# One store per output tile, a held-back score stretch and a last tile in three pieces

## The chip, the core and the metric

The kernel runs on one core of one Trainium2 chip. The core has TensorE (PE in the profile, with its weight loads as PEld), VectorE (DVE), ScalarE (ACT), GpSimd (POOL) and SyncE (SP), and 16 DMA engines. The metric is the device time of one execution in microseconds (us), lower is better. Before the change it is 586.98 us, the median of three runs (586.29 to 587.70).

## What is computed

Attention over 8 batches, 12 heads, 448 tokens and a head width of 64, with queries and keys divided by their root mean square and scaled by gains; then a mixer of rank 32 along the tokens; then a feed-forward layer along the 768 channels. All inputs and the output are 32-bit.

```
q_n, k_n = rmsnorm(q, g_q), rmsnorm(k, g_k)
attn = softmax(q_n @ k_n.T / 8)
x = (attn @ v) with the heads side by side        # 8 x 448 x 768
u = x + (x.T @ U @ V).T                            # U: 448 x 32, V: 32 x 448
out = u + relu(u @ w_ch1) @ w_ch2                  # 768 -> 3072 -> 768
```

## The kernel before, in words

**The work.** Matrix products take 16-bit operands. Twenty-four groups of four heads (`gi`, three to a batch) are loaded, normalised and turned so that the head width lies on the partitions. The last eighteen groups are turned by DMA transposes (`turn_dma`, L376), whose queries GpSimd then multiplies by the gains (`take_dma`, L383). A pair of heads (`pr`, six to a batch) has its scores and exponentials made by `Spair` (L422), in seven 128-key blocks: two blocks and one more each take a buffer of the PSUM pool `ps` (four buffers), two double blocks take the pool `ps_sc`. `V` (L448) multiplies by the values.

**The feed-forward part.** For each batch: `mix_t`, `mix_tr` and `mix_rows` (L479, L489, L525) make `u`, four DMA transposes (L548) bring it to `uT`, 24 `up` steps (L550) make `hT`, and `down` (L579) makes the output. A tile of output has 128 rows: two runs of 64 tokens, each at a stride of seven tokens in DRAM. It is made in two halves of 384 channels, each of 24 matmuls in four parts of six, and VectorE adds `u` to each half. A tile is stored by two DMAs of 64 rows each, half tile by half tile in the first batch and as whole rows of 768 after it. The last tile of the last batch is one of these: two halves, then two stores.

**The order.** It is laid down by a loop at the end of the kernel that merges two lists, the attention (`att`) and the feed-forward part (`mlp`), each entry with a cost. It keeps an estimate of the time at which each engine will be done (`at`, moved on by `runs`), and issues the next attention entry when its due time has come and `ready` (from L845) agrees. Engines take their instructions in this order. All loads of the attention, all stores and all DMA transposes go through SP's one DMA queue. A mixer step that would come directly behind a score stretch is moved behind a `down` part (`after_pair`).

**Single things that the steps below use.** `load_u` (L299) and the load of V (L304), whose DRAM side is V read four times over, for four groups of 32 partitions:

```
nc.sync.dma_start(Vf, moe_V.rearrange("(m r) s -> m r s", m=1).to_broadcast([NQ, rank, S]))   # NQ = 4
```

`sums` (L161) are two reductions on VectorE that the attention list puts into its queue once per group.

Of the kernel before, what the change touches and what calls it, by code (L numbers as in the profile page):

```python
# [9 lines left out]
FP32 = mybir.dt.float32  # L10
# [3 lines left out]
ALU = AluOpType  # L14
# [12 lines left out]
def kernel(  # L27
# [13 lines left out]
    nc = tc.nc  # L41
    B, H, S, D = q.shape
    dm = H * D
# [3 lines left out]
    P = 128  # L47
    NT = S // 64
    NJ = S // P
    SM = NJ * P  # L50
    R = S - SM
# [6 lines left out]
    KH = dh // P  # L58
    NPAIR = H // 2
    HALF = dm // 2  # L60
# [9 lines left out]
    outp = ctx.enter_context(tc.tile_pool(name="outp", bufs=3))  # L70
    ps_sc = ctx.enter_context(tc.tile_pool(name="ps_sc", bufs=2, space=bass.MemoryType.PSUM))
    ps = ctx.enter_context(tc.tile_pool(name="ps", bufs=4, space=bass.MemoryType.PSUM))
# [3 lines left out]
    for b in range(B):  # L76
        h = 0
# [194 lines left out]
    w2b = consts.tile([P, KH, dm], BF16)  # L272
    hT = consts.tile([P, KH, 512], BF16)
# [21 lines left out]
    Uf = first[:, 2, :2 * (NJ + 2) * rank].bitcast(FP32).rearrange("p (j r) -> p j r", r=rank)  # L295
    nc.gpsimd.memset(Uf[:, NJ:, :], 0.0)
    Urows = moe_U.rearrange("(p j) r -> p j r", j=NT)

    def load_u():  # L299
        for i in range(2):  # L300
            nc.sync.dma_start(Uf[i * R:(i + 1) * R, :NJ, :], Urows[:, i * NJ:(i + 1) * NJ, :])
        nc.sync.dma_start(Uf[R:P, NJ, :], Urows[:, 2 * NJ, :])
        nc.sync.dma_start(Uf[0:R, NJ + 1, :], Urows[:, 2 * NJ, :])
        nc.sync.dma_start(Vf, moe_V.rearrange("(m r) s -> m r s", m=1).to_broadcast([NQ, rank, S]))  # L304
# [32 lines left out]
    at = {"pe": 0.0, "act": 0.0, "dve": 0.0}  # L337
    exp_done = {}

    def runs(eng, us):  # L340
        at[eng] = us + (at["pe"] if eng == "pe" else max(at["pe"], at[eng]))

    qk, es, xs = {}, {}, {}
# [136 lines left out]
    def mix_t(b):  # L480

        pt = ps.tile([P, KD, rank], FP32, name="pu", tag="ps")
        for dt in range(KD):
            for j in range(NW):
                nc.tensor.matmul(pt[:, dt, :], xs[b][:, j, dt * P:(dt + 1) * P], Ub[:, j if j < NJ else NJ + b % 2, :],  # L485
                                 start=(j == 0), stop=(j == NW - 1))
        nc.vector.tensor_copy(tb_bufs[b % 2][:, :KD * rank], pt.rearrange("p k r -> p (k r)"))

    def mix_tr(b):  # L489
        pt = ps.tile([P, 2, P], BF16, name="pw", tag="ps")  # L490
        for i in range(2):
            nc.tensor.transpose(pt[:, i, :], tb_bufs[b % 2][:, i * P:(i + 1) * P], ident)
        tTs[b] = headp.tile([P, 2, P], BF16, name="tT", tag="tT")
        nc.vector.tensor_copy(tTs[b], pt)

    def mix_t0(lo, hi, scalar=False):

        pt = ps.tile([P, 512], FP32, name="pu0", tag="ps")
        for j in range(NW):
            nc.tensor.matmul(pt[:, :hi - lo], Uz[:, j, :], xs[0][:, j, lo:hi], start=(j == 0), stop=(j == NW - 1))  # L500
        if scalar:
            nc.scalar.copy(tz[:, lo:hi], pt[:, :hi - lo])
        else:
            nc.vector.tensor_copy(tz[:, lo:hi], pt[:, :hi - lo])
# [17 lines left out]
    def urows(b, col, half):  # L522
        h = slice(half * HALF, (half + 1) * HALF)
        return u_rest[:, h] if col == SM else xs[b][:, (col - (0 if b % 2 else R)) // P, h]
# [51 lines left out]

    down_ps, down_sb = {}, {}

    def down(b, col, half, part, nparts):  # L579
        key = (b, col, half)  # L580
        if part == 0:
            down_ps[key] = ps.tile([P, HALF], FP32, name="po", tag="ps")
        po = down_ps[key]
        n = KH // nparts
        for ht in range(part * n, (part + 1) * n):
            nc.tensor.matmul(po, hT[:, ht, col:col + P], w2b[:, ht, half * HALF:(half + 1) * HALF],  # L586
                             start=(ht == 0), stop=(ht == KH - 1))
        runs("pe", 0.98)
        if part < nparts - 1:
            return  # L590
        runs("dve", 0.55)
        h = slice(half * HALF, (half + 1) * HALF)
        if half == 0 or b == 0:
            down_sb[(b, col)] = outp.tile([P, dm], FP32, name="ob", tag="ob")
        ob = down_sb[(b, col)]
        nc.vector.tensor_tensor(ob[:, h], po, urows(b, col, half), ALU.add)  # L596
        if half == 1 or b == 0:
            h = h if b == 0 else slice(0, dm)

            def rows(b, j):  # L600
                return out[b].rearrange("(p j) d -> j p d", j=NT)[j]
            for i in range(2):
                o = rows(b, i * NJ + col // P) if col != SM else rows(b - i, 2 * NJ)
                nc.sync.dma_start(o[:, h], ob[i * R:(i + 1) * R, h])


    pairs = [(b, pr) for b in range(B) for pr in range(NPAIR)]
# [144 lines left out]
    mlp = []  # L752
    for b in range(B):
        for ht in range(KH):
            mlp.append((0.38, up_part, (b, ht, 4, KD), b) if b == 0 and ht < 2 else (1.14, up, (b, ht), b))
            if b < ROWS_FROM and ht % 2 == 0 and ht < 4 * NW:
                mlp.append((0.17, mix_rows, (b, ht // 4, ht // 2 % 2), b))
        cols = (64, 192, 320) if b % 2 == 0 else (384, 0, 128, 256)
        n = len(cols) * 8
        nb = b + 1  # L760
        pre = {}
        if ROWS_FROM <= nb < B:
            pre[n - PRE[nb > 1]] = [(0.77, mix_t, (nb,), nb)]
            pre[n - PRE[nb > 1] + 1] = [(0.11, mix_tr, (nb,), nb)]
            for piece in range(2 * NW):
                pre.setdefault(n - PRE[nb > 1] + 2 + (piece if nb > 1 else piece // 2), []).append(
                    (0.17, mix_rows, (nb, *divmod(piece, 2)), nb))
        tiles = [(col, half) for col in cols for half in range(2)]
        if b == 0:
            tiles.sort(key=lambda t: t[1])  # L770
        for c, (col, half) in enumerate(tiles):
            for part in range(4):
                mlp.extend(pre.get(c * 4 + part, []))
                mlp.append((0.98, down, (b, col, half, part, 4), b))

    a_, b_ = PARTS
    squares_part(0, *a_)
# [31 lines left out]
    sums(2, 0)  # L809
    stage_tiles(3)  # L810
    load_u()
    load_v(2)
    load_qk(3, 0)
# [28 lines left out]
    def mixes(f):  # L842
        return f in (mix_t, mix_tr, mix_rows)

    def ready(f, a):  # L845
        if f is Spair:
            return im == 0 or not mixes(mlp[im - 1][1])
        if ca >= a_one:
            return True
        if f is V:  # L850
            return exp_done[a[:2]] <= at["pe"] + 0.1
        return f is not Srows or at["act"] <= at["pe"] + 0.6

    later, turning, after_pair = [], False, False
    while ia < len(att) or im < len(mlp):
# [4 lines left out]
        if ia == a_from and im == 0:  # L860
            at.update(pe=0.0, act=0.0, dve=0.0)
        may_mlp = im < len(mlp) and ia >= done_at[mlp[im][3]]
        take_att = ia < len(att) and (not may_mlp or ca <= due(cm) and ready(*att[ia][1:]))
        if take_att:
            c, f, a = att[ia]
            if f is load:
                later.append((f, a))
            else:
                f(*a)
            after_pair = f is Spair or after_pair and f is not V  # L870
            if ia >= a_from:
                ca += c
            ia += 1
            if f is scale_all and a[0] < DMA_FROM:
                weights(2)
            if f is T and a == (DMA_FROM - 1, 1):
                nc.vector.memset(kp[:, 2 * NJ:], 0.0)
        else:
            if after_pair and mixes(mlp[im][1]):
                nb, n, moved = mlp[im][3], im, []  # L880
                while mixes(mlp[n][1]) and mlp[n][3] == nb:
                    e = next(i for i in range(n, len(mlp)) if mlp[i][1] is down)
                    moved += [mlp[e], *mlp[n:e]]
                    n = e + 1
                mlp[im:n] = moved
            after_pair = False
            c, f, a, _ = mlp[im]
            f(*a)
            turning = f is mix_t and a[0] > 0 or turning and a != (a[0], NW - 1, 1)
            cm += c  # L890
            im += 1
# [30 lines left out]
```

## Time and profile before

| what | value |
|---|---|
| median of three runs | 586.98 us (586.29 to 587.70) |
| the profiled execution's own time | 586.64 us |
| its span, first to last instruction | 584.8 us |
| PE busy | 572.2 us, 98% of the span |
| ACT, POOL, DVE busy | 307.9, 210.3, 196.8 us |
| moved by DMA | 68.21 MB, mean 117 GB/s |
| granted TensorE clock | 0.999 |

The page of the profile gives busy times, the span in 40 slices and the chain of work that ended last. The lists of waits say which engine stood idle and what ended it. The timeline shows instructions in order of time: start, length, engine, line, operation and how many were merged. The answer by windows gives for any stretch the busy time of each engine and, last, the mean busy share of the 16 DMA engines and the GB/s that they moved.

### The profile page before, as it was taken

Reading aid. Unit: us, or ns where it says so; the run is one execution under the profiler, and the core shown is the slowest. Engines: PE = TensorE matmul, PEld = TensorE weight load, DVE = VectorE, ACT = ScalarE, POOL = GpSimd, SP = SyncE. Lnnn points to the kernel's source line nnn. Section 1 sums busy time; section 2 is a strip of 40 time slices with the busy share of each in tenths; the row PEclk is TensorE's granted clock in tenths of the full one; section 3 lists DMA queues with packets and bytes.
Section 4 is the critical chain, followed back from the end, with each engine's and each line's share of the span. In section 5 each row is a group of like instructions: output and inputs, shape, how many; then the busy total and the mean of one; then the engine's idle time right before and its main releaser. Section 6 shows DMA issues by size and latency. Waiting matters only on the chain.

```text
span 584.8 us, 11725 instructions
## 1 busy us (share of the span) xinstructions
PE 572.2 (98%) x4826; PEld 338.2 (58%) x4826; DVE 196.8 (34%) x458; ACT 307.9 (53%) x510; POOL 210.3 (36%) x310
## 2 busy tenths in 40 slices
PE   8899999999999999999999999999999999999996
PEld 7555556555665555655556555665556655655563
DVE  6676656212352232521235231442034310410011
ACT  7866661677445776277653578457753344014200
POOL 5995684265314515334523433441531000000000
PEclk9999999999999999999999999999999999999999
DMA  8899999683546642585246735375204210420022
GB/s 229 170 241 241 244 233 231 119 220 52 133 78 167 153 106 35 139 212 130 36 122 109 180 104 123 66 172 149 35 25 92 48 28 1 68 61 1 1 54 55
DMA packets 104509, 68.21 MB, mean 117 GB/s; under 512 B 66568, under 2 KB 101256, under 8 KB 104456
## 3 DMA queue, kind: packets, MB, share of 16 engines
q1 hardware_dynamic: 95044, 58.03, 42.6%
q0 software_dynamic: 9408, 9.44, 9.6%
q8 instruction: 38, 0.62, 0.4%
q14 instruction: 15, 0.12, 0.1%
q10 hardware_dynamic: 4, 0.00, 0.0%
HBM read 52.20 MB, written 11.01 MB: 108 GB/s over the span
## 4 chain that ended last, share of the span: by engine, by line
PE 91%; DMA 3%; DVE 2%; POOL 1%; ACT 1%; issue 1%; SPq 1%; POOLq 0%; ACTq 0%
PE ph L554 36%; PE po L586 36%; PE pv L466 6%; PE sc L436 2%; PE sl L427 2%; PE sl L438 2%; PE pv L462 2%; PE pm L537 2%; DMA qf<-in_q_dram 1%; PE sc L415 1%; ACT E L416 1%; DMA vf<-in_v_dram 1%; DVE ssq L162 1%; DMA qT<-qn 1%; PE pu L485 1%
## 5 line engine op out<-in xcount | busy, mean ns | idle before, releaser
L586 PE MATMUL po<-w2b,hT 128*128 128x384 bf16 x1344 | 237.4, 326 | 0.0
L554 PE MATMUL ph<-uT,w1b 128*128 128x448 bf16 x1140 | 228.7, 352 | 0.0
L586 PEld LDWEIGHTS <-hT 128*128 128x128 bf16 x1344 | 126.8, 98 | 75.5 <-issue 0.6
L554 PEld LDWEIGHTS <-w1b 128*128 128x128 bf16 x1140 | 108.3, 98 | 93.8 <-issue 0.7
L561 ACT ACTIVATE hT<-ph 128x448 bf16<-128x448 f32 x184 | 98.0, 550 | 120.2 <-PE ph L554 118.9
L429 ACT ACTIVATE E<-sl,gg 128x448 bf16<-128x448 f32 x72 | 41.5, 629 | 75.9 <-PE sl L427 75.9
L386 POOL TENSOR_SCALAR qT<-qT,gg 128x448 bf16<-128x448 bf16 x36 | 50.5, 1402 | 81.6 <-DMA qT<-qn 65.2
L193 POOL TENSOR_TENSOR qn<-qf,rs 128x384 bf16<-128x384 f32 x36 | 29.9, 829 | 132.4 <-ACT rs L170 127.5
L469 DVE RECIPROCAL r<-pv 128x4 f32<-128x4 f32 x96 | 17.4, 182 | 167.8 <-PE pv L466 167.6
L441 ACT ACTIVATE E<-sc,gg 128x896 bf16<-128x896 f32 x72 | 69.0, 1022 | 0.0
L596 DVE TENSOR_TENSOR ob<-po,x 128x384 f32<-128x384 f32 x48 | 26.7, 557 | 103.8 <-PE po L586 103.4
L466 PE MATMUL pv<-va,E 128*128 128x65 bf16 x1152 | 57.1, 194 | 0.0
L466 PEld LDWEIGHTS <-E 128*128 128x128 bf16 x1152 | 50.5, 98 | 6.3
L162 DVE TENSOR_REDUCE ssq<-sq 128x14 f32<-128x896 f32 x45 | 46.8, 1078 | 2.4 <-ACT sq L140 2.3
L462 PE MATMUL pv<-vl,E 128*128 128x130 bf16 x192 | 42.2, 220 | 0.3 <-ACT E L416 0.2
L470 DVE TENSOR_TENSOR x<-pv,r 128x256 bf16<-128x256 f32 x96 | 40.7, 424 | 3.3
L416 ACT ACTIVATE E<-sc,gg 128x896 bf16<-128x896 f32 (+1 forms) x42 | 37.5, 950 | 4.1 <-PE sc L415 4.1
L542 DVE TENSOR_TENSOR x<-pm,x 128x384 bf16<-128x384 f32 x48 | 26.2, 552 | 16.5 <-PE pm L537 14.2
L193 POOL TENSOR_TENSOR kp<-kf,rs 128x384 bf16<-128x384 f32 x36 | 29.8, 828 | 0.0
L169 ACT ACTIVATE rs<-ssq,eps 128x28 f32<-128x28 f32 (+1 forms) x25 | 7.8, 314 | 33.4 <-DVE ssq L162 29.2
L462 PEld LDWEIGHTS <-E 128*128 128x128 bf16 x192 | 18.7, 97 | 9.7 <-issue 2.0
L439 ACT ACTIVATE E<-sl,gg 128x448 bf16<-128x448 f32 x36 | 22.9, 637 | 0.0
(102 smaller groups left out, 387.9 us busy)
## 6 DMA issues: line engine op xcount, KB each, us to landing
qf<-in_q_dram SPq DMA_DIRECT2D x23, 448.0 KB, 3.7
kf<-in_k_dram SPq DMA_DIRECT2D x23, 448.0 KB, 6.4
out_dram<-ob SPq DMA_DIRECT2D x50, 192.0 KB, 2.8
vf<-in_v_dram SPq DMA_DIRECT2D x48, 192.0 KB, 5.9
w1b<-in_moe_w_ch_dram POOLq DMA_DIRECT2D x4, 1152.0 KB, 19.8
w2b<-in_moe_w_ch_dram POOLq DMA_DIRECT2D x8, 576.0 KB, 17.7
vf<-in_v_dram SPq DMA_DIRECT2D x48, 32.0 KB, 5.7
out_dram<-ob SPq DMA_DIRECT2D x12, 96.0 KB, 3.6
```

The source lines that it names most:

```text
L162: nc.vector.tensor_reduce(ssqs[gi][:, i, :], sqs.pop((gi, i)), AX, ALU.add)
L193: nc.gpsimd.tensor_tensor(main.rearrange("p (t i) d -> p i t d", i=2), src[:, c, :2 * NJ].rearrange("p (i t) d -> p i t d", i=2), rs[:, c, ...
L386: nc.gpsimd.tensor_scalar(qT[:, a], qT[:, a], gg[:, 0:1], None, ALU.mult)
L416: nc.scalar.activation(es[(b, pr)][:, 2 * r:2 * r + n, :], sc[:, :n, :S], AF.Exp, scale=scal, bias=bias)
L429: nc.scalar.activation(E[:, 4 + i, :], ts[i], AF.Exp, scale=scal, bias=bias)
L441: nc.scalar.activation(E[:, 2 * r:2 * r + 2, :], tiles[r][:, :, :S], AF.Exp, scale=scal, bias=bias)
L462: nc.tensor.matmul(pv[:, i].rearrange("p e d -> p (e d)"), E[:, 2 * NJ, w:w + P], vl[:, lp, :], start=True, stop=False)
L466: nc.tensor.matmul(pv[:, i, e, :], E[:, 2 * j + e, w:w + P], va[:, (first_h + step * e) * NJ + j, :], start=False, stop=(e == 1 and j == N ...
L470: nc.vector.tensor_tensor(xs[b].rearrange("p i (h d) -> p i h d", d=D)[:, 2 * half:2 * half + 2, h0:h0 + step + 1:step, :], pv[:, :, :, :D ...
L554: nc.tensor.matmul(ph, w1b[:, dt, ht * P:(ht + 1) * P], uT[:, dt, off:off + S], start=(dt == 0), stop=(dt == KD - 1))
L561: nc.scalar.activation(hT[:, ht, off:off + S], ph, AF.Relu)
L586: nc.tensor.matmul(po, hT[:, ht, col:col + P], w2b[:, ht, half * HALF:(half + 1) * HALF], start=(ht == 0), stop=(ht == KH - 1))
```

## The change

The loads of U for the first 6/7 of its rows become one DMA instead of two. Each output tile that is not the small-remainder tile is stored by one DMA, whose DRAM side is written as two runs of 64 rows and whose SBUF side has 128 partitions. The estimates of `mix_t` and `mix_tr` are entered into `at`. A score stretch (`Spair`) is issued only when VectorE is estimated to be at most 0.3 us and ScalarE at most 1.0 us behind PE. The last tile of the last batch is made in three accumulations, of 384, 256 and 128 channels, each with its own add and its own store.

```
-        for i in range(2):
-            nc.sync.dma_start(Uf[i * R:(i + 1) * R, :NJ, :], Urows[:, i * NJ:(i + 1) * NJ, :])
+        nc.sync.dma_start(Uf[:, :NJ, :], Urows[:, :2 * NJ, :].rearrange("p (i j) r -> i p j r", i=2))
...
+        runs("pe", 0.62)
+        runs("dve", 0.35)
...
+        runs("pe", 0.11)                      # mix_tr
+        runs("dve", 0.3)
...
+    def store(b, col, h, ob):
+        def rows(b):
+            return out[b].rearrange("(p j) d -> j p d", j=NT)
+        if col == SM:
+            for i in range(2):
+                nc.sync.dma_start(rows(b - i)[2 * NJ, :, h], ob[i * R:(i + 1) * R, h])
+        else:
+            nc.sync.dma_start(rows(b)[col // P:col // P + NJ + 1:NJ, :, h], ob[:, h])
+
+    ENDS = (HALF, 5 * P, dm)
+
+    def down_end(b, col, piece):
+        lo, hi = (0, HALF) if piece == 0 else ENDS[piece - 1:piece + 1]
+        if piece == 0:
+            down_sb[(b, col)] = outp.tile([P, dm], FP32, name="ob", tag="ob")
+        ob = down_sb[(b, col)]
+        po = ps.tile([P, HALF], FP32, name="po", tag="ps")[:, :hi - lo]
+        for ht in range(KH):
+            nc.tensor.matmul(po, hT[:, ht, col:col + P], w2b[:, ht, lo:hi], start=(ht == 0), stop=(ht == KH - 1))
+        nc.vector.tensor_tensor(ob[:, lo:hi], po, xs[b][:, col // P, lo:hi], ALU.add)
+        store(b, col, slice(lo, hi), ob)
...
-            def rows(b, j):
-                return out[b].rearrange("(p j) d -> j p d", j=NT)[j]
-            for i in range(2):
-                o = rows(b, i * NJ + col // P) if col != SM else rows(b - i, 2 * NJ)
-                nc.sync.dma_start(o[:, h], ob[i * R:(i + 1) * R, h])
+            store(b, col, h, ob)
...
+        if b == B - 1:
+            tiles = tiles[:-2]
...
+    mlp.extend((3.9 * w, down_end, (B - 1, cols[-1], piece), B - 1) for piece, w in enumerate((1.0, 0.67, 0.34)))
...
         if f is Spair:
-            return im == 0 or not mixes(mlp[im - 1][1])
+            if im > 0 and mixes(mlp[im - 1][1]):
+                return False
+            return at["dve"] <= at["pe"] + 0.3 and at["act"] <= at["pe"] + 1.0
```

## The prediction

> **What bounds the kernel now.** I read the page first, then PE's own waits, then the timeline around each wait and around the end, then DMA shares by windows. PE is busy 98% of the span and makes 91% of the chain that ended last:
>
> ```profile
> span 584.8 us, 11725 instructions
> ...
> PE 572.2 (98%) x4826; PEld 338.2 (58%) x4826; DVE 196.8 (34%) x458; ACT 307.9 (53%) x510; POOL 210.3 (36%) x310
> ...
> PE 91%; DMA 3%; DVE 2%; POOL 1%; ACT 1%; issue 1%; SPq 1%; POOLq 0%; ACTq 0%
> ```
>
> So an edit saves only what PE waits for, or the tail behind PE; and whatever makes PE wait costs in full. PE's list of waits has three rows of `Spair` lines (columns: total us, times, longest):
>
> ```profile
> PE sl L427 <- POOL qT L386: 1.1, 1, 1.1
> ...
> PE sl L438 <- DVE tb L487: 0.6, 1, 0.6
> PE sl L427 <- DVE x L542: 0.5, 1, 0.5
> ```
>
> That is 2.2 us, all that holding score stretches back can win.
>
> **The stretches held back.** With the new rule 12 of the 36 `Spair` calls come later, by one to four `mlp` entries; the amount of PE work is the same. By the timeline, the waits lie at pairs (2,2), (3,2) and (5,2), and all three calls move. At (3,2) PE waited for VectorE, which had two reductions (2.07 us) queued ahead of the mixer's adds; the stretch now comes two `down` parts later, when its PSUM buffers are long free: -0.5 us, and a trace of 0.1 at (4,2). At (5,2) the order becomes `mix_t`, one `down` part, `mix_tr`, with the stretch behind them. `mix_tr` needs the copy `tb`, which stands behind the same two reductions and ends at 303.93 us, while PE's `down` part ends at 302.5. So PE waits 1.4 us there instead of 0.65: +0.8 us. Behind it only PE's own queue waits. At (2,2) PE waited for the turned queries, and one more `up` (1.14 us) now comes first, which would hide the 1.1. The other eight had no wait, and I find none in front of the buffers that they get. Together, (2,2) left aside: +0.2 us.
>
> **The stores, SP's part.** An issue takes SP 0.47 to 0.60 us whatever its size, so a tile saves SP about 0.55 us. SP's queue matters at one place, around 100 us (below); elsewhere nothing behind it is late.
>
> **The stores, the DMA engines' part.** Here I read the windows (columns: window, length, five engines' busy time, clock, DMA share, GB/s):
>
> ```profile
> 19.75:19.90 0.15, 0.15 (x10) 0.15 (x7) 0.15 (x1) 0.00 (x0) 0.15 (x1) 1.00 0.25 96
> 580.50:581.55 1.05, 0.00 (x0) 0.00 (x0) 0.00 (x0) 0.00 (x0) 0.00 (x0) 1.00 0.00 0
> 581.60:582.40 0.80, 0.00 (x0) 0.00 (x0) 0.00 (x0) 0.00 (x0) 0.00 (x0) 1.00 1.03 223
> 104.00:107.00 3.00, 3.00 (x21) 1.43 (x20) 0.56 (x1) 1.61 (x4) 0.20 (x1) 1.00 0.69 153
> ```
>
> The first is the load of V (L304, issued at 17.72 us) with no other transfer's data in it: its share is 0.25 and its rate 96 GB/s, so four of 16 engines work, at 24 GB/s each, and its DRAM side begins with a dimension of four. The third is the last pair of 64-row stores: all engines, 223 GB/s. The new store's DRAM side begins with a dimension of two. **By the row nearest in shape it gets two engines, 48 GB/s.** The ends are 48 and 223 GB/s; I take 48, since V's SBUF side has 128 partitions as the new store's has, and its DRAM side alone set the four. A tile of 393 KB then takes 8.2 us on two engines instead of 1.7, a half tile of the first batch 4.1.
>
> The Trainium skill, DMA: Bandwidth & Descriptors, section "Why a DMA increments its semaphore by 16 and not by 1", says that a DMA issued from SP runs on the largest number of engines up to 16 that divides the slowest dimension of both sides. For V that is 4, as the window shows; for the new store it would be 2, and the sum would be the one below.
>
> Everything else on SP's queue is spread over all engines and done only when the slowest two are, so loads and transposes issued behind a store wait for it on those two. Twenty-four tiles take this form. From 120 us on, the turned queries are ready 4 us or more before their stretch (256 us for the stretch at 260, 315.6 for the one at 324) and mostly 10 to 19; I work them out at about no wait, +1 us at most each at (3,4) and (4,4). Two places are tight.
>
> **Place one, 86 to 116 us.** SP's rows (S0 to S4 are half-tile stores, two issues each):
>
> ```profile
> 85.92 1.18 SPq L604 DMA_DIRECT2D out_dram<-ob  x2
> ...
> 97.69 3.03 SPq L604 DMA_DIRECT2D out_dram<-ob  x4
> 101.36 4.44 SPq L548 DMA_TRANSPOSE uT<-x  x3
> 105.88 1.22 SPq L548 DMA_TRANSPOSE uT<-u_rest  x1
> 107.19 2.46 SPq L604 DMA_DIRECT2D out_dram<-ob  x4
> 109.76 1.56 SPq L378 DMA_TRANSPOSE qT<-qn  x1
> ```
>
> and PE's:
>
> ```profile
> 111.07 3.57 PE L554 MATMUL ph<-uT,w1b 128*128 128x448 bf16 x18
> 115.72 0.37 PE L427 MATMUL sl<-qT,kT 64*128 64x448 bf16 x2 [1.08 <-POOL qT L386]
> ```
>
> A half tile puts 98 KB on each of two engines instead of 12 KB on each of 16: 86 KB more, 3.6 us at 24 GB/s. Three lie ahead of the `uT` transposes: +10.7. Those now run back to back: between 104 and 107 us SP issued one each 1.24 us and the share was 0.69, so one takes 0.86, and four give back 1.5. The last landed at 105.88 + 2.4 (its row among the DMA issues) = 108.3, and now at 117.5. The first `up` of batch 1 needs it: it starts at 117.5 instead of 111.07, and four end at 122.1. The queue then holds S3 and S4 (8.2 us, to 125.3), the transpose of the queries (0.86, and 0.4 to land) and GpSimd's scaling (1.41): 128.0. The stretch (2,2) waits until then. Before it started at 115.72 with three `up` done; with the fourth that is 116.86. **+11.1 us.** SP's two saved issues cannot help a queue that the engines hold. Bounds: nothing if SP's other transfers do not wait behind a store; +15 if S0, which also meets the weight loads (share 1.31 from 83 to 95 us), costs two times as much. PE then stands for some 6 us twice; the first 72 matmuls of 128 columns took 6.70 us, 93 ns each instead of the 56 of later ones, so a cold clock could add up to 3 us.
>
> **Place two, the end.** PE's 48 matmuls of the last tile become 72 with the same columns. Later matmuls of 128 columns follow each other at 56 to 60 ns with a new weight each, so +0.1 us, hidden here.
>
> The Trainium skill, TensorE: Matmul & The Clock Gate, section "Back-to-back issue gap", gives about 81 ns for a sustained stream of weight load and 128-column matmul; that would be an estimated 0.5 us more, and the trace's 65-column products at 31 ns with a weight load each speak against it.
>
> If all 16 engines served the stores, the last add would shrink from 0.56 to about 0.29 us (384 channels 0.56, 256 elements 0.42), one issue of 0.52 us and most of the packets would go: about -1 us. On two engines: VectorE ends tiles 0 and 128 at 564.84 and 572.64. The second window shows 1.1 us from issue to data, so tile 0 moves from 566.0 to 574.2, tile 128 to 582.4, the three pieces of the last tile, all issued by then, to 590.6; landed at 591.0. Before, the last store was issued at 581.0 and landed 2.6 us later, at 583.6. **+7.4 us**; bounds +5 (its packets of 3072 bytes at 25 GB/s an engine, no gaps) and +9 (the short rows of the pieces dearer).
>
> U's load on two engines moves 49 KB in 1 us, needed 10 us later: nothing.
>
> **Sum.** 11.1 + 0.2 + 7.4 = +18.7 us, on the profiled execution's own 586.64: 605.3. That execution lies 0.3 under the median of the runs, 586.98; against it I say **605.5 us** (+3.2%).
>
> **Rivals.**
> - *All engines serve the new stores.* For it: SBUF's side has 128 partitions, and every store so far ran on all. Against: V's share of 0.25. Then the waits give -1.1 at (2,2) and +0.2, the end -1.0: 585.1, faster. It decides wholly: with 223 GB/s no queue forms. The price is 20 us between the two sides, the place is the first dimension of one access pattern. Chance 0.10.
> - *Two engines, but only the end pays*, because transposes and loads get past a store on its engines, or place one has slack that I don't see: -1.1 + 0.2 + 7.4 gives 593.5. For it: SP's transposes were limited by their issue, not by the engines. Against: one queue. Chance 0.20.
> - *The stores on all engines, but the new wait at (5,2) and others like it eat the rest*: 586.5, no change. Chance 0.02.
> - The forecast: 0.66, from 597 to 613; above that 0.02.
>
> The 80% range holds the forecast and the second rival: 591 to 613. About 0.2% is what a measurement of this kernel can tell from no change. Faster 0.10, same 0.02, slower 0.88.
>
> **What would show it.** In the profile after: a DMA share near 0.13 and some 50 GB/s behind the last matmul, for about 10 us; PE waits for a DMA of `uT` at batch 1's first `up` and for POOL's `qT` at (2,2); a wait of `pw` for `tb` at (5,2) of 1.4 us, none of `sl` for `x`; the three pieces' adds 0.56, 0.42 and 0.29 us. A share near 1 in the last window, or a last landing within 3 us of the last add, proves the forecast wrong.

## The result, and the profile after

The changed kernel takes **620.56 us** (median of six runs, 617.65 to 623.15), the kernel before 586.85 beside it: a ratio of 1.0578, with a 95% interval of 1.0544 to 1.0612. The prediction was 605.5 us, with a range of 591 to 613. The direction and the main mechanism, stores on two engines, were right; what they hold up was worked out too small at two places, and the time lies outside the range.

The profiled execution took 621.15 us. From the page of the changed kernel, span, busy times and the engines' shares of the chain that ended last:

```profile
span 619.2 us, 11754 instructions
...
PE 578.9 (93%) x4850; PEld 340.9 (55%) x4850; DVE 196.7 (32%) x459; ACT 309.1 (50%) x510; POOL 209.8 (34%) x310
...
PE 81%; DMA 9%; ACT 2%; POOL 2%; DVE 1%; SPq 1%; issue 1%; POOLq 0%; DVEq 0%; ACTq 0%
```

PE no longer bounds the whole span: it stands still for 7% of it, and DMA makes 9% of the chain, where it made 3%. The other engines' work is the same to 1.5 us. PE's 6.7 us more of busy time are no more work: PE issues the same columns, some at half clock, as seen below.

PE's list of waits in the changed kernel (total us, times, longest), the rows that bear on the change:

```profile
PE sl L426 <- POOL qT L385: 11.9, 3, 5.9
PE sl L437 <- DVE ob L621: 4.8, 1, 4.8
PE po L611 <- DMA w2b<-in_moe_w_ch_dram: 3.3, 2, 1.8
...
PE pw L493 <- DVE tb L486: 1.3, 1, 1.3
```

In the kernel before, three rows of score stretches summed to 2.2 us. Now the turned queries alone (`qT`) cost 11.9, at three places, and there are two waits that the prediction did not have: for an output buffer (`ob`) and for a weight load (`w2b`).

Behind the last matmul, which starts at 606.0, the windows of the changed kernel (window, length, five engines, clock, DMA share, GB/s) read:

```profile
605.00:610.00 5.00, 1.23 (x23) 1.05 (x19) 0.64 (x2) 0.00 (x0) 0.00 (x0) 0.84 0.13 52
610.00:615.00 5.00, 0.00 (x0) 0.00 (x0) 0.00 (x0) 0.00 (x0) 0.00 (x0) 0.50 0.13 49
```

A share of 0.13 is two of 16 engines, at 25 GB/s each. The kernel before had 1.03 and 223 GB/s at its end.

### The profile page after: what moved, and what is told of

It reads as the page before. It is cut to its first block, busy times and chain, and to the rows that moved or that the text cites. A ratio compares the mean times of both kernels' runs of the same rounds, so it can differ in the third digit from the quotient of the medians.

```text
span 619.2 us, 11754 instructions
## 1 busy us (share of the span) xinstructions
PE 578.9 (93%) x4850; PEld 340.9 (55%) x4850; DVE 196.7 (32%) x459; ACT 309.1 (50%) x510; POOL 209.8 (34%) x310
## 3 DMA queue, kind: packets, MB, share of 16 engines
q0 software_dynamic: 9408, 9.44, 10.1%
## 4 chain that ended last, share of the span: by engine, by line
PE 81%; DMA 9%; ACT 2%; POOL 2%; DVE 1%; SPq 1%; issue 1%; POOLq 0%; DVEq 0%; ACTq 0%
PE ph L557 33%; PE po L611 30%; DMA qT<-qn 7%; PE pv L465 5%; PE sc L435 2%; PE sl L426 2%; PE pv L461 2%; PE sl L437 2%; DMA out_dram<-ob 1%; PE pm L540 1%; PE po L600 1%; ACT E L415 1%; PE sc L414 1%; DMA kf<-in_k_dram 1%; POOL qT L385 1%
## 5 line engine op out<-in xcount | busy, mean ns | idle before, releaser
L611 PE MATMUL po<-w2b,hT 128*128 128x384 bf16 x1296 | 231.7, 328 | 3.3 <-DMA w2b<-in_moe_w_ch_dram 3.3
L557 PE MATMUL ph<-uT,w1b 128*128 128x448 bf16 x1140 | 232.3, 356 | 0.2
L611 PEld LDWEIGHTS <-hT 128*128 128x128 bf16 x1296 | 122.9, 98 | 81.4 <-issue 10.4
L426 PE MATMUL sl<-qT,kT 64*128 64x448 bf16 x72 | 13.5, 369 | 11.9 <-POOL qT L385 11.9
```

Source lines behind the costliest of these rows:

```text
L557: nc.tensor.matmul(ph, w1b[:, dt, ht * P:(ht + 1) * P], uT[:, dt, off:off + S], start=(dt == 0), stop=(dt == KD - 1))
```

## Where the time came from

`two_stores`, the first experiment below, is the changed kernel with two stores for each tile. Its PE issues the same matmuls in the same order, so each matmul's start in one trace can be taken from its start in the other. The changed kernel's delay grows at the five places of the table and at the end, and nowhere else:

| place | delay added, us | of it a stop of PE | of it half clock behind the stop |
|---|---|---|---|
| two waits for `w2b`, 97 to 102 us | 3.6 | 3.6 | 0 |
| pair (2,0), output buffer, 110 to 122 | 7.7 | 5.2 | 2.6 |
| pair (2,2), turned queries, 126 to 137 | 7.4 | 5.1 | 2.3 |
| pair (3,4), turned queries, 213 to 223 | 6.3 | 3.5 | 2.8 |
| pair (4,4), turned queries, 283 to 285 | 2.5 | 2.5 | 0 |
| from the start of the last matmul to the end (13.2 for 4.1) | 9.1 | | |

The stop is the delay that a matmul's start adds at one step, and the half clock what the matmuls behind it add while they run slow. The 5.2 us at (2,0) include 0.3 for `uT` at the first `up`; at (2,2) the 0.8 us that `two_stores` also waits is taken off. The sum is 36.6 us, and the medians differ by 620.56 - 583.95 = 36.6. Against the kernel before, the same execution's last matmul is 26.5 us later and the end behind it 7.9 us longer.

The half clock is read from the windows of the changed kernel; the third column from the right is the granted clock:

```profile
112.50:115.00 2.50, 0.08 (x1) 0.08 (x1) 0.56 (x1) 0.00 (x0) 0.00 (x0) 0.69 0.13 50
115.00:117.50 2.50, 2.50 (x12) 1.24 (x12) 0.00 (x0) 2.01 (x3) 0.00 (x0) 0.50 0.13 50
117.50:120.00 2.50, 2.50 (x20) 1.49 (x18) 0.61 (x2) 2.09 (x3) 0.00 (x0) 0.50 1.04 209
```

PE stood from 110.1 to 114.9, and then works on at 0.50 until about 120: it is busy all the while, at half speed. The first line also shows that two engines alone are at work (0.13, 50 GB/s) while PE waits.

## The experiments

Pieces that were taken back or done alone come first, then the batches apart, then single mechanisms, then a version that beats both kernels. "Before" is the kernel before, run on the same chip.

**Two stores again.** The changed kernel with

```
-            nc.sync.dma_start(rows(b)[col // P:col // P + NJ + 1:NJ, :, h], ob[:, h])
+            for i in range(2):
+                nc.sync.dma_start(rows(b)[i * NJ + col // P, :, h], ob[i * R:(i + 1) * R, h])
```

> The changed kernel with each output tile stored by two DMAs of 64 rows again; the hold-back rule, U's single load and the three last pieces (two stores each) stay. Theory (a store whose DRAM side begins with two runs serves only two DMA engines, and all that is lost comes from that): about 586, from 584.5 to 586.9; the prediction's steps other than the stores give -1.1 at the pair (2,2), +0.2 for the other stretches and about -0.3 at the end, and the waits of 11.9 us for turned queries and of 4.8 us for the output buffer are gone. Rival (the held-back stretches themselves come too late or meet full buffers, and the slow stores cost only the end): about 612, with most of those waits still there.

Measured: 583.95 us, 0.9955 of before (0.994 to 0.997). The theory holds and the rival falls: what is left of the change makes the kernel 2.6 us faster. PE's waits for `w2b` and `ob` are gone and that for `qT` is 0.8.

**The stores alone.** The kernel before with one DMA for each tile, by the same `store`.

> The kernel before with one edit: one DMA for each output tile. Theory: all of the loss is there, 619 to 623, DMA share near 0.13 behind the last matmul, waits for w2b, for turned queries, and of VectorE's adds for an output buffer. Rival (the rule's order is what makes the turned queries late): about 595, the 8 us of the end alone.

Measured: 619.61 us, 1.0561 (1.0542 to 1.0581). All of the loss is there, as the theory said, without the new rule: 13.1 us of waits for `qT`, 1.6 for `w2b`, 3.3 for the output buffer.

**The rule alone.** The kernel before with the four `runs` lines of `mix_t` and `mix_tr` and the new last lines of `ready`.

> The kernel before with the hold-back rule for score stretches and the estimates of mix_t and mix_tr alone. Theory, by the prediction's steps: 585.9 (585.5 to 586.9); the wait for turned queries at (2,2) of 1.1 us gone, those of (3,2) and (4,2) gone, a wait of 1.4 us for tb at (5,2) in place of 0.65. Rival (the rule makes stretches late): 590 or more, with new waits of PE on ScalarE or of V on the exponentials.

Measured: 585.54 us, 0.9981 (0.9969 to 0.9993), 1.1 us faster; the theory holds but for one wait. Of PE's waits in this kernel two lines bear on it:

```profile
PE pw L494 <- DVE tb L487: 1.3, 1, 1.3
PE sl L427 <- DMA kT<-kp: 0.7, 1, 0.7
```

The first is the wait for `tb` at (5,2), 1.3 us where 1.4 was worked out; the waits for `x` and for `sl` behind `tb` are gone. The second is at (2,2): with the fourth `up` ahead of it the stretch still waits 0.7 us of the 1.1, since the turned operands came 0.5 us later in this execution.

**The three pieces alone.** The kernel before with `down_end`, each piece stored by two DMAs.

> The kernel before with the last tile in three accumulations alone, each stored by two DMAs of 64 rows. PE's order is otherwise that of before. Theory: -0.3 (586.0 to 587.2): the last add is 0.29 us instead of 0.56, and six issues of 0.5 us stand on SP where two stood, of which the last two follow the last add as before. Rival (the issues of the earlier pieces hold up the last ones on SP, and the 24 added weight loads cost PE): +0.5 to +1.5.

Measured: 585.10 us, 0.9981 (0.9964 to 0.9997), about 1.1 us faster and more than the 0.3 expected: from the start of the last matmul to the end 4.0 us instead of 5.3. The six issues do not stand in each other's way.

**Which batches pay.** The changed kernel, with the single store in batch 0, in batches 1 to 6, or in batch 7 alone (`elif b > 0:` and the like ahead of the two stores).

> The changed kernel with two stores for each tile of batches 1 to 7, and one store for each half tile of batch 0. Theory (batch 0's slow stores make all the waits up to 137 us): the waits that the changed kernel shows there, 3.6 us for w2b, 5.0 at the pair (2,0), 0.3 at the first up and 6.1 at (2,2), 15 us in all, and some 4 us of half clock behind the two long ones: 584 + 19 = 603 (599 to 606). Rival (the prediction's own working: only uT and the turned queries of (2,2) are late, 11 us): 595, with a wait of 6 us for uT and none for w2b or the output buffer.

Measured: 603.14 us, 1.0304 (1.0277 to 1.0331), with waits of 5.9 for `qT`, 4.3 for `ob` and 2.2 for `w2b`, where 3.6 had been taken over from the changed kernel: the theory holds. The prediction's own place one would have been 595.

> The changed kernel with one store for each whole tile of batches 1 to 6 alone, two for those of batches 0 and 7. Theory (their stores delay the transposes of the queries by themselves): waits of 3.6 us at (3,4) and 2.6 at (4,4) and some 2 us of half clock, 584 + 8 = 592 (589 to 594). Rival (those two waits come from SP's queue still being late from batch 0): 584 to 585, with no wait there.

Measured: 594.03 us, 1.0135 (1.0113 to 1.0157), and 594.12 in a second set of runs:

> The kernel with slow stores in batches 1 to 6 alone, issued by SP, beside the other on the same chip: 594, waits of 6.9 us for turned queries.

There it was 1.0126 (1.0096 to 1.0156). The theory holds: 5.0 us of delay at (3,4) and 4.7 at (4,4) arise with batch 0 undisturbed; in the second trace 3.3 and 4.7, since there no half clock follows the stop at (3,4).

> The changed kernel with one store for each tile of the last batch alone. Theory: the end alone is longer, by the 8.0 us that the changed kernel shows between the last matmul and the end, and by up to 0.7 less that the pieces had won: 592 (591 to 593). Rival (the end is longer because the queue comes late to it): 584 to 586.

Measured: 593.10 us, 1.0121 (1.0102 to 1.014). The end is 13.2 us long, as in the changed kernel; the theory holds. By the traces the three add 17.3, 9.5 and 9.1 us to `two_stores`, 35.9 of the 36.6.

**The first dimension.** One store for a tile, but to 128 rows at one stride (the remainder's rows are moved likewise):

```
-            nc.sync.dma_start(rows(b)[col // P:col // P + NJ + 1:NJ, :, h], ob[:, h])
+            nc.sync.dma_start(out[b][:SM].rearrange("(p j) d -> j p d", j=NJ)[col // P, :, h], ob[:, h])
```

> The changed kernel with one store for each tile, but to 128 rows at one stride of three rows, so that its DRAM side begins with one dimension of 128. It writes the tiles' rows to other places of the output than the reference does; the bytes, the rows' length and the number of DMAs are those of the changed kernel. Theory (the first dimension of two sets the number of engines): all 16 engines, no queue, 583 to 584.5, a share near 1 behind the last matmul. Rival (a store of 128 partitions in one DMA is slow by itself, by its size or by its single issue): about 620, with the changed kernel's waits.

Measured: 583.11 us, 0.9954 (0.9937 to 0.997). Its windows, of the middle piece's store and of the last:

```profile
575.50:576.00 0.50, 0.50 (x7) 0.44 (x6) 0.00 (x0) 0.00 (x0) 0.00 (x0) 1.00 0.89 332
...
579.10:579.40 0.30, 0.00 (x0) 0.00 (x0) 0.00 (x0) 0.00 (x0) 0.00 (x0) 1.00 0.72 212
```

The same bytes in the same number of DMAs run on all engines at 212 to 332 GB/s. So it is not the single DMA, nor its size: it is that its DRAM side begins with a dimension of two. Nor is it the stride, which is three rows here and seven in the changed kernel: the stores of the kernel before have the seven too, and ran at 223 GB/s. This is the prediction's reading. It is also what the Trainium skill, DMA: Bandwidth & Descriptors, section "Why a DMA increments its semaphore by 16 and not by 1", states; here 2 gave 0.13, 4 (the load of V) 0.25 and 128 up to 0.89.

**The output buffer.** Batch 0's slow stores, with both halves of a tile in one buffer (`if half == 0 or b == 0:` became `if half == 0:`), so that no add of batch 0 waits for a store.

> The kernel with slow stores in batch 0 alone, but with both half tiles of a tile in one output buffer, so that no add of batch 0 waits for a store. Theory (the queue is the bound, the buffer only the place where PE meets it first): VectorE's wait of 9.6 us for out_dram and PE's of 4.3 at (2,0) go, PE then waits for uT at batch 1's first up, and the time stays within 2 us of 603: 601 to 604. Rival (the output buffer costs by itself): 4.3 us and some 2 us of half clock are won, 597.

Measured: 602.91 us, 1.0252 (1.0214 to 1.0291), beside 603.14 of the same kernel without this edit. The theory holds. PE's waits in this kernel:

```profile
PE ph L557 <- DMA uT<-u_rest: 7.0, 1, 7.0
PE po L614 <- DMA w2b<-in_moe_w_ch_dram: 3.7, 2, 1.9
PE sl L426 <- POOL qT L385: 3.5, 1, 3.5
```

The wait for `ob` is gone, and 7.0 us for `uT` at batch 1's first `up` stand in its place. That is the wait that the prediction had worked out (117.5 - 111.07 = 6.4). In the changed kernel PE met another effect of the same queue some microseconds earlier and was late enough not to see it.

**The half clock.** Batch 0's slow stores, with `keep_busy(108)` ahead of the stretch (2,2).

> The kernel with slow stores in batch 0 alone, with 108 products of two 128 by 128 tiles, which nothing reads, ahead of the stretch (2,2), where PE stood for 6 us. Theory (the half clock behind the stop comes from the stop): the granted clock stays 1.00 behind it, and about 1.9 us of the 603.1 go: 601.2. Rival (the clock is lowered by something else there): 603, the clock at 0.50 for 5 us as before.

Measured: 601.24 us, 1.0228 (1.0199 to 1.0256). The windows of this kernel behind the covered stop:

```profile
130.00:132.50 2.50, 2.50 (x37) 1.82 (x35) 0.00 (x0) 0.60 (x2) 2.50 (x2) 1.00 1.09 321
132.50:135.00 2.50, 2.50 (x15) 1.27 (x13) 0.00 (x0) 2.50 (x5) 2.50 (x6) 1.00 1.12 274
```

The clock stays at 1.00 where the kernel without the added products has 0.50, though the stretch still waits for its queries. The medians differ by 1.9 us as expected and the profiled spans by 1.8 (599.6 and 597.8); the ratios, to other runs of before, differ by 0.0076, which would be 4.5 us, so the size is less sure than the sign. By the traces the half clock behind this stop costs 2.5 us in `one_in_b0`, and the covered stretch starts 0.8 us later, which leaves the 1.8. In all four executions the mean granted clock is 0.994 to 0.997, beside 0.989 to 0.992 without the products. The half clock comes from the stop, and it can be covered.

**Queue or engines.** Batch 0's stores from ScalarE's queue (`nc.scalar.dma_start`).

> The kernel with slow stores in batch 0 alone, each issued from ScalarE's queue instead of SP's; the shape of the stores and the two engines stay. Theory (transposes and loads wait because they stand behind the store in SP's queue): most of the 19 us goes, 585 to 592, without a wait for turned queries at (2,2); ScalarE pays 0.6 us for each issue and its wait for the add. Rival (the two engines themselves are the bound, whichever queue): 600 to 604, with the same waits.

Measured: 598.91 us, 1.0197 (1.0164 to 1.023), neither one nor the other. No stretch waits for turned queries, but PE waits 4.0 and 5.0 us for ScalarE, which stands at its store issues. The same for batches 1 to 6:

> The kernel with slow stores in batches 1 to 6 alone, each issued from ScalarE's queue instead of SP's; shape and engines of the stores stay. There whole tiles are stored, and ScalarE has 0.6 us of issue and a short wait for each add. Theory (the transposes wait because they stand behind the store in one queue): the waits of 6.9 us for turned queries and the half clock go, 584 to 587. Rival (the two engines are the bound, whichever queue feeds them): 592 to 595, with waits for turned queries at (3,4) and (4,4).

Measured: 612.83 us, 1.0439 (1.0395 to 1.0483), far worse than either expectation. PE's waits for turned queries fall from 6.9 to 0.4 us, but ScalarE's list of waits shows it standing behind SP's transfers:

```profile
ACT hT L564 <- DMA vf<-in_v_dram: 9.5, 1, 9.5
...
ACT hT L564 <- DMA qT<-qn: 8.1, 1, 8.1
ACT hT L564 <- DMA kT<-kp: 6.8, 1, 6.8
```

The named `hT` steps do not read these tiles. It is the store ahead of them that waits: by the semaphores that the trace names, the DMAs of SP and ScalarE share eight, taken in turn, and each DMA waits for the one issued eight before it. So an engine that issues one store waits for other engines' transfers, and its own work stands behind. That the turned queries are not late speaks for the order in SP's queue, and so do SP's own rows: the median issue of a `uT<-x` transpose takes SP 1.25 us in the kernel before, 2.91 in the changed kernel, 2.78 in `one_in_mid`, and 1.25 again here. So behind a slow store of its own queue SP stands at the issue itself, and behind one from ScalarE's queue mostly not. But 8.4 us of waits for `uT` stand at two first `up` steps of this kernel. Both runs bring a cost of their own, so whether the engines would hold the transposes back without the queue stays open.

**A version that beats both.** `two_stores`, with `mix_tr` and what follows moved behind one more `down` part where VectorE is late, and the last store from ScalarE:

```
+                eng = nc.scalar if i and h.start == ENDS[1] else nc.sync
...
-            if after_pair and mixes(mlp[im][1]):
+            late = mlp[im][1] is mix_tr and at["dve"] > at["pe"] + 0.3
+            if (after_pair or late) and mixes(mlp[im][1]):
```

> The changed kernel with two stores for each tile, with mix_tr and what follows it moved behind one more down part where VectorE is estimated to be over 0.3 us behind PE (two batches), and with the second store of the last piece issued by ScalarE. Theory (the wait of 1.3 us for tb is a matter of order, and SP's last issue of 0.5 us stands on the path): 1.3 and 0.5 less than the 584.0 of two stores: 582.2 (581.5 to 583.4), no wait of pw for tb. Rival (the mixer's steps come too late for the transposes, or the wait moves to another buffer): 584 or more.

Measured: 583.06 us, 0.9922 (0.9899 to 0.9944), 4.6 us below before by the ratio and 0.9 below `two_stores` by the medians, within the expected range. The wait of `pw` for `tb` is gone. The timeline of its end:

```profile
577.14 0.29 DVE L603 TENSOR_TENSOR ob<-po,x 128x128 f32<-128x128 f32 x1 [0.91 <-PE po L602]
577.46 0.55 ACTq L591 DMA_DIRECT2D out_dram<-ob  x1
```

ScalarE issues its store right behind the last add, beside SP. The intervals of this kernel and of `two_stores` overlap by 0.0004 and rest on different runs of before, so the 0.9 us between them is likely, not certain.

## Why the prediction was wrong, point by point

- **What bounds the kernel; only PE's waits and the tail count.** Right. The table above accounts for all 36.6 us with PE's stops, the clock behind them and the tail.
- **The stretches held back, +0.2 and -1.1 at (2,2).** Right in sum: -0.9 worked out, -1.1 measured (`only_rule`). Only the cover of the wait at (2,2) was too hopeful.
- **Two engines, 48 GB/s.** Right: 49 to 52 GB/s, share 0.13. The rival with all 16 engines was priced at 585.1, and `two_stores` and `one_of_128`, which are that case, gave 583.95 and 583.11.
- **Place two, +7.4.** Right: 7.9 us against the kernel before. The three adds took 0.56, 0.43 and 0.29 us. (The lower bound of +5 does not follow from the rate beside it: three tiles at 50 GB/s take 23.6 us, which gives +6.4.)
- **Place one, +11.1: mis-sized.** It cost 18.7 us, the first three rows of the table. The bounds that the prediction gave itself, +15 and up to 3 for a cold clock, reach 18, but the sum took neither. The term that was mis-sized is S0, put at 3.6 us like the two other stores ahead of `uT`. SP's rows behind S0 in the kernel before:

```profile
87.21 1.72 SPq L378 DMA_TRANSPOSE qT<-qn  x1
89.45 1.21 SPq L380 DMA_TRANSPOSE kT<-kp  x1
```

  and in the changed kernel:

```profile
86.09 3.91 SPq L377 DMA_TRANSPOSE qT<-qn  x1
90.11 4.15 SPq L379 DMA_TRANSPOSE kT<-kp  x1
...
105.54 1.99 SPq L589 DMA_DIRECT2D out_dram<-ob  x2
107.64 10.63 SPq L551 DMA_TRANSPOSE uT<-x  x3
118.37 1.21 SPq L551 DMA_TRANSPOSE uT<-u_rest  x1
...
120.90 3.95 SPq L377 DMA_TRANSPOSE qT<-qn  x1
```

  SP takes 12.7 us to issue the four transposes behind S0, where it took 5.4, and S1 and S2, whose adds were done by 95.3, go out at 105.54 instead of 97.69. So S0 cost 7.8 us, as in the upper bound; why it costs two times 3.6 no run shows. From there on the prediction's steps fit: it has 16.2 us from the issue of S1 to the first `up`, and the trace 16.3 (to 121.88). The last `uT` transpose, worked out to land at 117.5, is only issued at 118.4, and the stretch (2,2) was to start at 128.0 and starts at 132.5. Behind it come 2.3 us of half clock, which I had only as a bound; and 0.7 us is that `two_stores` reaches this stretch at 116.19, where the prediction counted from 116.86.

  PE meets the late queue at two places that the prediction did not have. The weight loads land later (`w2b` 22.0 us after its issue by the median, 17.7 before), and PE waits 3.6 us for them; that S0 on its two engines slows them is argued, but the wait is there only with batch 0's slow stores. And a slow store keeps its output buffer, of which there are three. VectorE's list of waits has it:

```profile
DVE ob L621 <- DMA out_dram<-ob: 10.1, 1, 10.1
```

  VectorE's add stood 10.1 us for a store to land, the PSUM buffer behind it stayed taken, and PE met that before it met `uT`. By `b0_own_halves` this moves the wait and adds nothing: there the stretch (2,2) starts 17.8 us later than in `two_stores`, of which that execution had lost 1.4 before batch 0's stores, and in the changed kernel 16.3. The queue's lateness is the price, paid once.
- **Elsewhere from 120 us on, "+1 us at most each at (3,4) and (4,4)": wrong.** This is the step that failed outright: 6.3 and 2.5 us in the changed kernel, and 9.5 for batches 1 to 6 by themselves. I had set the slack of the turned queries against one slow store. At (3,4) two of them add up. In `two_stores` the first half's queries are turned and scaled at 187.8 us for a stretch at 194.75, a slack of 6.9. In the changed kernel PE is 18.6 us late there, so they would be ready at 206.4; they are at 216.85, 10.4 later, and 10.4 - 6.9 is the stop of 3.5 us. The windows of the changed kernel show how:

```profile
203.00:205.00 2.00, 2.00 (x17) 1.00 (x12) 0.00 (x0) 1.95 (x4) 0.00 (x0) 1.00 1.07 223
...
211.00:213.00 2.00, 2.00 (x12) 1.07 (x11) 0.93 (x1) 1.18 (x3) 0.00 (x0) 1.00 0.13 49
213.00:215.00 2.00, 0.43 (x3) 0.00 (x0) 0.00 (x0) 0.97 (x3) 0.00 (x0) 1.00 1.38 65
```

  A store issued at 185.6 holds the two engines (0.13 at 193 to 195), so `uT`'s transposes and the next group's loads come late and still run at 203 to 205 on all engines. The store issued at 202.5 comes behind them, holds the two engines until 213, and the transposes, issued from 203.2 on, end only behind it. A backlog that is not worked off before the next slow store is handed on.
- **The rivals.** "Only the end pays" (593.5) is refuted for the whole; it is what batch 7 alone costs (593.10). The signs that I named came out, except the wait for `uT`, which is 0.3 us here and shows in full only in `b0_own_halves`.
- **U's load, nothing.** No run tried it alone. `two_stores` kept it and gained, so it costs little at most.

Taken together, the sum was +18.7 where the spans of the two profiles differ by 34.3: 7.6 us short at place one, 8.8 at (3,4) and (4,4), 0.5 at the end, and 1.2 too high at the rule (+0.2 worked out, -1.0 between the last matmuls of `two_stores` and the kernel before), which fits to 0.1. Of the delay at place one and at (3,4), 7.7 us are half clock.

## What to carry to other kernels

Before two DMAs are merged into one, look at the first dimension of both sides: a merge that puts a dimension of two in front took two of 16 engines, and two DMAs of 64 rows were 36.6 us faster than one. Where a slow transfer is put into a queue, follow the queue on to the next slow one, and follow the buffer that it holds as well; slack counts against the backlog of all of them, not against one. And price a stop of PE of some three microseconds or more at its length and, in most cases here, about 1.6 to 2.8 us of half clock behind it.

## What the runs showed of the hardware

- **Half clock behind a stop.** In the changed kernel, behind idle times of PE of 3.5, 4.8 and 5.9 us the granted clock was 0.50, and matmuls ran slow for 4.8 to 5.8 us, at a loss of 2.3 to 2.8 us; behind 1.5, 1.8 and 2.5 us it stayed at 1.00. The length of the stop alone does not decide it: in `one_in_mid` 2.9 us was enough, for a loss of 1.7, and in `only_store` 2.3 us (0.53 at 285 to 287.5 us) and even two stops of 1.6 and 0.6 us close together (0.50 at 103 to 105 us), while in `one_in_mid_again` the clock stayed at 1.00 behind 3.25 us (197.5 to 202.5 us). The Trainium skill, TensorE: Matmul & The Clock Gate, section "Part 1: The HAM clock gate (the "warmup" mystery)", puts both the idle and the busy stretch at about 3.4 us; the traces agree in kind, with drops behind shorter stops and slow stretches of some 3 to 6 us.
- **A DMA share far above 1.** Windows in which the two engines had a backlog show shares of 1.38 to 3.46 at 65 to 72 GB/s (207 to 209 and 213 to 215 us). I take it that the time of packets that stand behind others is counted too; no run tried it. There the GB/s tell what moves.
